# Attention scores as three 32-row products beside the up projection, a turn to the values every two key tiles, and a geglu stage in a written order

## The chip, the cores and the metric

The kernel runs on one core of a Trainium2 chip. The metric is the device time of one execution in microseconds (us). Before the change, three runs took 1081.52, 1082.40 and 1082.88 us; their median is 1082.4.

## The reference

Two branches read the same x (2048 tokens of 448 numbers), and a gate g per token mixes them.

```
q, k, v = split(x @ wqkv)                 # 16 heads of 28
a = softmax(q @ k.T * 28**-0.5) @ v @ wo
b = (gelu(x @ w_gate) * (x @ w_up)) @ w_down      # hidden width 1792
g = sigmoid((x * gate_w).sum(-1, keepdims=True))
out = g * a + (1 - g) * b
```

## The kernel before, in words

All large products but the values' are made in three pieces: each operand is split into a high part (fp32r, TensorE's fast form of fp32) and a low part, and high x high, high x low and low x high are summed. UNITS (line 46) lists the 21 products of 64 rows of which one block of x @ w consists (x has 448 columns: seven pieces of 64 rows, three products each). A block is 128 outputs by 512 tokens.

The program has three stages.

*First* (lines 88 to 265): x, wqkv and the gate vector are loaded and split; q and k are computed and stored to HBM as high and low parts (qkd), v stays in SBUF as V, and per head a shift that keeps exp in range goes to shd. A few warm-up products on zeros (WARM, line 113) run ahead. Then a flag is read and a branch (line 295) is passed that these inputs don't take.

*Attention* (lines 267 to 503): for each head h and each of 16 tiles of 128 keys (kt), two half score tiles of 128 keys by 1024 queries are made. `scores` (line 356) fills a PSUM tile sc (three buffers of two banks) with two 512-column chunks. Q and K of a head lie in SBUF twice, on rows 0 to 63 and on rows 64 to 127: K has high and low part stacked in 28 rows each and a few rows of ones, so one 64-row product makes (K high + K low) x Q high and a second one x Q low. That is four 64-row products per half. ScalarE takes exp of sc into pt (line 378). Four value products per key tile and half pair (`values`, line 381) multiply pt by V, each on its own strip of 32 columns of TensorE, in plain fp32, which the profile shows as two passes each.

Beside the scores the same loop computes x @ w_up, and the first part of x @ w_gate, in blocks of 21 products on one half of the rows (`product`, `unit`, `start`); the result goes from PSUM (psu, one buffer) by a VectorE copy (two buffers u) to HBM (ud). NOUT is the number of blocks made in this stage; a block's half of the rows alternates from block to block. `run` (line 350) writes the order in which the two halves get their products, so that two of them can lie side by side. RATE is the largest number of up products for one half tile. After a block, `hold` keeps the next one back for a few half tiles so that its copy can finish. ENDS and LATE set when the loop turns to the values: a group ends at the key tiles in ENDS, and its values are run when LATE half tiles of the next group are done; then hold is 0 again. Two blocks are made ahead of the loop and two behind it (`two_blocks`), side by side in one score tile. The next head's Q and K are loaded at key tile 2 of each head, all on SP's DMA queue.

*Geglu* (lines 506 to 631): the hidden width is cut in 14 pieces of 128 (ORDER), two to a chunk. `hidden` makes, for each piece and pair of token blocks, the w_gate product if it isn't made yet (pg), then gelu on ScalarE, times u on VectorE, then the split into high and low part hl. `down` multiplies by w_down into pd, and VectorE adds (1 - g) times the result to acc (lines 573 to 578). The projection of the attention output by wo (`project`) is put between. In this stage most instructions of ScalarE, VectorE and SP are placed by the framework's scheduler; only TensorE's products have the order in which they are written (`mm` pins them).

Of the kernel before, what the change touches and what calls it, by code (L numbers as in the profile page):

```python
# [17 lines left out]
P = 128  # L18
# [9 lines left out]
ENDS = (3, 7, 11, 15)  # L28
LATE = 3
RATE = 4  # L30
NOUT = 68
# [4 lines left out]
WARM = 9  # L36
LAG = 6
NR = 2 * DH
# [15 lines left out]
def gated_mix(ctx: ExitStack, tc: tile.TileContext, xT, wqk, wvg, wg, wu, wd, wo, sel, ident, out):  # L54
# [26 lines left out]
    def both(dst, src, mark=lambda ins: ins, eng=None):  # L81

        for g in range(2):
            mark((eng or nc.sync).dma_start(out=dst[side(g), 0:4], in_=src[0:64]))
            mark((eng or nc.sync).dma_start(out=dst[side(g), 4:7], in_=src[64:128, 0:3]))


    with ExitStack() as ph:
# [37 lines left out]
        def load():  # L126
            nonlocal issued
            if issued == len(loads):
                return
            a, r = loads[issued], raws[issued % AHEAD]  # L130
            k = int(a[-1])
            for g in range(2):
                eng = nc.scalar if a in ("x00", "x02") else nc.sync
                if a[0] == "a":
                    src, n = wqk[k, 0:64], TB
                elif a[0] == "b":
                    src, n = wqk[k, 64:128, 0:3 * P], 3 * P
                elif a[0] == "x":
                    src, n = xT[int(a[1]) + 2 * g, side(k // 4), k % 4], TB
                else:  # L140
                    src, n = wvg[side(k // 4), k % 4], VW
                pin(eng.dma_start(out=r[side(g), 0:n], in_=src))
            issued += 1
# [126 lines left out]
    heads = [(kq.tile([P, 2, S], F32R, name=f"Q{i}"), kq.tile([P, S], F32R, name=f"K{i}")) for i in range(2)]  # L270
    for Q, K in heads:
        for g in range(2):
            edge = slice(64 * g + 32, 64 * g + 64)
            pin(nc.gpsimd.memset(K[edge].bitcast(F32), 1.0))
            pin(nc.gpsimd.memset(Q[edge].bitcast(F32), 0.0))

    def load_q(dst, h):
        for a in range(2):
            for g in range(2):
                for j in range(2):  # L280
                    at = 64 * g + j * DH
                    nc.sync.dma_start(out=dst[at:at + DH, a].bitcast(F32), in_=qkd[a, h * DH:(h + 1) * DH])

    def load_k(dst, h):
        for g in range(2):
            for a in range(2):
                at = 64 * g + a * DH
                nc.sync.dma_start(out=dst[at:at + DH].bitcast(F32), in_=qkd[a, D + h * DH:D + (h + 1) * DH])
# [41 lines left out]
    with ExitStack() as ph:  # L330
        pp = ph.enter_context(tc.tile_pool(name="pp", bufs=11))
# [7 lines left out]
        def load_head(h):  # L339
            Q, K = heads[h % 2]  # L340
            if h:
                load_k(K, h)
                load_q(Q, h)
            for g in range(2):
                nc.sync.dma_start(out=Q[64 * g + NR:64 * g + NR + 2, 0].bitcast(F32), in_=shd[h])


        free = [0, 0]

        def run(todo):  # L350
            while todo[0] or todo[1]:
                g = min((g for g in range(2) if todo[g]), key=lambda g: free[g])
                todo[g].pop(0)()
                free[g] = max(free[g], free[1 - g] - 1) + 1

        def scores(h, kt, half, n):
# [3 lines left out]
            todo = [[], []]  # L360
            n = min(n, left())
            if n:

                f = block["g"]
                todo[f] += [unit] * n
                to = (1 - f, 1 - f if n > 1 else f)
            else:
                f = min(range(2), key=lambda g: free[g])
                to = f, 1 - f
            for c in range(2):  # L370
                g = to[c]
                for a in range(2):
# [8 lines left out]
        def values(h, kt):  # L381
            if kt == 0:
                PO[h] = pso.tile([P, 512], F32, name="po")
# [38 lines left out]
        def product(block):  # L422
# [4 lines left out]
            if block["n"] == len(UNITS):  # L427
                u = op.tile([P, TB], F32, name="u")
                nc.vector.tensor_copy(u, block["p"])  # L429
                nc.sync.dma_start(out=block["out"], in_=u)  # L430
# [11 lines left out]
        def unit():  # L442
# [3 lines left out]
            if block["n"] == len(UNITS):  # L446
                hold = 3

        def two_blocks():

            sc = psc.tile([P, 1024], F32, name="sc")
            todo = []
            for g in range(2):
                start(sc[:, g * 512:(g + 1) * 512])
                b = dict(block)
                todo.append([lambda b=b: product(b)] * len(UNITS))
            block["n"] = len(UNITS)
            run(todo)
# [40 lines left out]
        hold = 0  # L499
        while left():  # L500
            unit()
            hold = 0
# [3 lines left out]
    with ExitStack() as ph:  # L506
        ap = ph.enter_context(tc.tile_pool(name="ap", bufs=1, reuse_waits="tile"))
        acc = ap.tile([P, NT, D], F32, name="acc")
        hp = ph.enter_context(tc.tile_pool(name="hp", bufs=8, reuse_waits="tile"))
# [7 lines left out]
        def load_f(f):  # L517
            if any((1, f, tb) not in made for tb in range(NTB)):
                if (1, f) not in halves:
                    load_half(1, f, by_act)  # L520

            hi, lo = 0, TB
            w = gp.tile([P, 2 * TB], F32R, name="w", bufs=3)
            draw = gp.tile([P, TB], F32, name="draw")[:, 0:D]
            nc.sync.dma_start(out=draw, in_=wd[f * P:(f + 1) * P])
            hi, lo = w[:, hi:hi + D], w[:, lo:lo + D]
            nc.scalar.activation(hi, draw, AF.Copy)  # L527
            nc.vector.tensor_tensor(lo, draw, hi.bitcast(F32), OP.subtract)
            WD[f] = hi, lo

        def hidden(f, b):

            us, pgs, hls = [], [], []
            for tb in (b, b + 2):
                s = slice(tb * TB, (tb + 1) * TB)
                u = tp.tile([P, TB], F32, name="u")
                nc.sync.dma_start(out=u, in_=ud[0, f, :, s])
                us.append(u)
                if (1, f, tb) in made:
                    pg = tp.tile([P, TB], F32, name="gs", bufs=2)  # L540
                    nc.sync.dma_start(out=pg, in_=ud[1, f, :, s])
                else:
                    pg = psg.tile([P, TB], F32, name="pg")
                pgs.append(pg)
# [122 lines left out]
```

## Time and profile before

The profiled execution took 1081.29 us; its span, from the first to the last instruction, is 1079.5 us.

| engine | busy us | share of the span |
|---|---|---|
| TensorE products | 1047.9 | 97% |
| TensorE weight loads | 733.0 | 68% |
| ScalarE | 612.3 | 57% |
| VectorE | 332.9 | 31% |
| GpSimd | 69.2 | 6% |

How to read the rows: PE is a TensorE product, PEld a weight load (it overlaps products), DVE is VectorE, ACT ScalarE, POOL GpSimd, SP the engine that issues most DMAs. A group's row gives line, engine, operation, out<-in and count, then the busy time of the group in us and the mean of one in ns, then the idle time of the engine just ahead of them with what ended it. All products have line 60, so the tile's name tells them apart: sc scores, pu up blocks, po values, pg w_gate, pd the second product and the projection. Products are pipelined: one of 512 columns is shown 0.39 us long while the next starts much earlier, so the distance between starts is the price, and "busy" is not work at full rate. A timeline row gives start and length in us.

### The profile page before, as it was taken

What the parts mean: (1) busy time and instruction counts of PE and PEld (TensorE: products, weight loads), DVE (VectorE), ACT (ScalarE), POOL (GpSimd) and SP (SyncE); (2) the same over time, 40 slices, a digit from 0 to 9 for tenths busy, and PEclk for the clock granted to TensorE, in tenths of its full rate; (3) what the DMA queues carried; (4) which work ended last, traced back from release to release, by engine and by line L of the source; (5) the groups of instructions that cost most, each with busy time, mean ns of one, the idle gap of its engine ahead of it and who ended that gap; (6) DMA issues with size and microseconds to landing.
All of it is one profiled execution on the core that took longest, in us unless ns stands there. A gap on an engine that the chain in (4) does not pass through costs nothing.

```text
span 1079.5 us, 20134 instructions
## 1 busy us (share of the span) xinstructions
PE 1047.9 (97%) x8257; PEld 733.0 (68%) x8257; DVE 332.9 (31%) x515; ACT 612.3 (57%) x740; POOL 69.2 (6%) x47
## 2 busy tenths in 40 slices
PE   8999799999999999999999999999888999999997
PEld 6889555655665665565566556556576889888886
DVE  4552112111111111111111111111287656646644
ACT  5332377777777877777787777778344304131320
POOL 3524200000000000000000000000001011100000
PEclk9999899999999999999999999999998999999999
DMA  6795544345345344344354444422476314122313
GB/s 188 250 380 148 133 115 134 106 124 138 103 128 144 89 134 137 102 126 132 101 141 118 111 135 114 123 81 67 152 208 199 103 57 120 49 59 80 105 49 137
DMA packets 68321, 138.19 MB, mean 128 GB/s; under 512 B 15744, under 2 KB 25984, under 8 KB 62784
## 3 DMA queue, kind: packets, MB, share of 16 engines
q1 hardware_dynamic: 67904, 136.33, 42.8%
q8 instruction: 66, 1.08, 0.4%
q10 hardware_dynamic: 320, 0.52, 0.2%
q14 instruction: 31, 0.25, 0.1%
HBM read 96.44 MB, written 40.37 MB: 127 GB/s over the span
## 4 chain that ended last, share of the span: by engine, by line
PE 77%; DMA 4%; ACT 3%; DVE 3%; issue 2%; SPq 0%; DVEq 0%; ACTq 0%
PE po L60 21%; PE sc L60 21%; PE pu L60 16%; PE pd L60 11%; PE pg L60 8%; ACT pt L378 2%; DMA out<-gs 1%; DMA u<-ud 1%; DVE ohl L601 1%; DMA oraw<-in_wo 1%; DVE gs L578 1%; DMA oraw<-od 1%; DMA draw<-in_wd 1%; DVE g L554 0%; DMA gs<-ud 0%
## 5 line engine op out<-in xcount | busy, mean ns | idle before, releaser
L378 ACT ACTIVATE pt<-sc 128x1024 f32<-128x1024 f32 x512 | 477.7, 1041 | 170.6 <-PE sc L60 169.5
L60 PE MATMUL sc<-Q,K 64*128 64x512 f32 x2048 | 413.8, 399 | 0.6 <-ACT pt L378 0.4
L60 PEld LDWEIGHTS sc<-Q,K 64*128 64x128 f32 x2048 | 314.5, 184 | 83.3 <-issue 50.3
L60 PE MATMUL pu<-X,half 64*128 64x512 f32 x1344 | 317.4, 387 | 0.0
L60 PEld LDWEIGHTS pu<-X,half 64*128 64x128 f32 x1344 | 247.1, 184 | 33.9 <-issue 1.7
L60 PE MATMUL po<-pt,V 128*32 128x512 f32 x2048 | 234.4, 598 | 0.0
L60 PE MATMUL pd<-w,hl 128*128 128x448 f32 x672 | 145.5, 373 | 9.8 <-DVE acc L575 5.0
L60 PEld LDWEIGHTS po<-pt,V 128*32 128x32 f32 x2048 | 60.2, 110 | 139.5 <-issue 135.8
L429 DVE COPY u<-pu 128x512 f32<-128x512 f32 x64 | 43.8, 685 | 348.9 <-PE pu L60 289.4
L60 PEld LDWEIGHTS pd<-w,hl 128*128 128x128 f32 x672 | 126.4, 190 | 28.1 <-DVE acc L575 6.2
L60 PE MATMUL pg<-X,half 64*128 64x512 f32 x924 | 106.9, 388 | 0.0
L60 PEld LDWEIGHTS pg<-X,half 64*128 64x128 f32 x924 | 88.1, 184 | 18.5 <-issue 2.7
L60 PE MATMUL pq<-X,WQK 64*128 64x512 f32 x588 | 69.2, 394 | 3.1 <-ACT X L161 2.5
L60 PEld LDWEIGHTS pq<-X,WQK 64*128 64x128 f32 x588 | 56.1, 188 | 16.4 <-ACT X L161 3.3
L527 ACT ACTIVATE w<-draw 128x448 fp32r<-128x448 f32 x14 | 8.1, 578 | 92.8 <-PE pd L60 70.2
L575 DVE SCALAR_TENSOR_TENSOR acc<-pd,gate,acc 128x448 f32<-128x448 f32 x80 | 52.8, 681 | 17.0 <-PE pd L60 16.9
L599 POOL CAST ohl<-oraw 64x512 fp32r<-64x512 f32 x4 | 2.4, 606 | 800.2 <-DMA oraw<-od 698.9
L555 ACT ACTIVATE hl<-g 128x512 fp32r<-128x512 f32 x56 | 33.9, 629 | 24.8 <-DVE g L554 20.6
L554 DVE TENSOR_TENSOR g<-g,u 128x512 f32<-128x512 f32 x56 | 36.7, 687 | 33.3 <-ACT g L553 28.5
L556 DVE TENSOR_TENSOR hl<-g,hl 128x512 fp32r<-128x512 f32 x56 | 36.7, 689 | 9.2 <-ACT hl L555 8.3
L553 ACT ACTIVATE g<-pg 128x512 f32<-128x512 f32 x44 | 24.1, 593 | 26.3 <-PE pg L60 26.3
L60 PE MATMUL pd<-WO,ohl 128*128 128x448 f32 x176 | 36.7, 367 | 0.0
(65 smaller groups left out, 449.2 us busy)
## 6 DMA issues: line engine op xcount, KB each, us to landing
Q<-qkd SPq DMA_DIRECT2D x128, 224.0 KB
ud<-u SPq DMA_DIRECT2D x68, 256.0 KB
qkd<-hl SPq DMA_DIRECT2D x28, 512.0 KB
K<-qkd SPq DMA_DIRECT2D x64, 224.0 KB
u<-ud SPq DMA_DIRECT2D x56, 256.0 KB
rb<-rdend SPq DMA_DIRECT2D x64, 64.0 KB
hraw<-in_wu SPq DMA_DIRECT2D x28, 128.0 KB
od<-o SPq DMA_DIRECT2D x64, 56.0 KB
```

Source lines behind the costliest of these rows:

```text
L60: return pin(nc.tensor.matmul(o, lhsT, rhs, start=start, stop=stop))
L378: nc.scalar.activation(pt, sc, AF.Exp, scale=SCALE)
L429: nc.vector.tensor_copy(u, block["p"])
L527: nc.scalar.activation(hi, draw, AF.Copy)
L553: nc.scalar.activation(g, pg, AF.Gelu_apprx_tanh)
L554: nc.vector.tensor_tensor(g, g, u, OP.mult)
L555: nc.scalar.activation(hl[:, 0], g, AF.Copy)
L556: nc.vector.tensor_tensor(hl[:, 1], g, hl[:, 0].bitcast(F32), OP.subtract)
L575: nc.vector.scalar_tensor_tensor(acc[:, t], p, g1, acc[:, t], OP.mult, OP.add)
L578: nc.vector.scalar_tensor_tensor(y, p, g1, acc[:, t], OP.mult, OP.add)
L599: nc.gpsimd.tensor_copy(O[0:64, 3], o[0:64, 3])
L601: nc.vector.tensor_tensor(O[64:, 3], o[64:, 3], O[64:, 3].bitcast(F32), OP.subtract)
```

## The change

- **Scores.** Q and K are laid out anew: on each quarter of 32 rows K has its high part in one plane and its low part in another (`[P, 2, S]`), and Q holds high and low part for the 512-query chunks of its quarter. A 512-column chunk of scores is three 32-row products (K high x Q high, K low x Q high, K high x Q low) on one quarter; the two chunks take the two quarters of one half of the rows, and the up products the other half. `run` orders three lists by quarters. Six products per half tile take the place of four.
- **Loop.** ENDS is every second key tile, so the values are run for two key tiles at a time, twice as often; LATE is 2 half tiles, RATE 3 up products. The first half tiles of head 0 get one more. `two_blocks` ahead of the loop is gone; behind the loop the unfinished block and one more run side by side, their copies are issued behind both, then come the last values. NOUT is 66 instead of 68. pt has 8 buffers instead of 11.
- **Geglu.** All instructions of the stage are pinned. The parts hl have one place per piece and token block. The gate's tail (gelu, times u, split) is cut into steps; `down` and `project` run one step of waiting side work between the product and the sum of each tile, and the weights, u and gate inputs of the next chunk are prepared in the second half of a chunk. w_down pieces have 4 buffers instead of 3. The split of the attention output moves from GpSimd to ScalarE and VectorE, piece by piece.
- **Elsewhere.** 12 warm-up products instead of 9; loads that went to both halves of the rows as two DMAs are one DMA with a broadcast source; fewer and smaller GpSimd memsets.

The core of the diff (the weights, wo and w_down loads and most of the pins are left out):

```diff
-ENDS = (3, 7, 11, 15)
-LATE = 3
-RATE = 4
-NOUT = 68
+ENDS = tuple(range(1, 16, 2))
+LATE = 2
+RATE = 3
+NOUT = 66
-WARM = 9
+WARM = 12
...
-    heads = [(kq.tile([P, 2, S], F32R, name=f"Q{i}"), kq.tile([P, S], F32R, name=f"K{i}")) for i in range(2)]
+    heads = [(kq.tile([P, 2, 2, TB], F32R, name=f"Q{i}"), kq.tile([P, 2, S], F32R, name=f"K{i}")) for i in range(2)]
...
     def load_q(dst, h):
         for a in range(2):
-            for g in range(2):
-                for j in range(2):
-                    at = 64 * g + j * DH
-                    nc.sync.dma_start(out=dst[at:at + DH, a].bitcast(F32), in_=qkd[a, h * DH:(h + 1) * DH])
+            for g in range(4):
+                nc.sync.dma_start(out=dst[quarter(g, DH), a].bitcast(F32), in_=queries(qkd[a, h * DH:(h + 1) * DH], g))
...
-        free = [0, 0]
+        free = [0] * 4
 
         def run(todo):
-            while todo[0] or todo[1]:
-                g = min((g for g in range(2) if todo[g]), key=lambda g: free[g])
-                todo[g].pop(0)()
-                free[g] = max(free[g], free[1 - g] - 1) + 1
+            todo = [(q, list(p)) for q, p in todo if p]
+            now = 0
+            while todo:
+                q, p = min(todo, key=lambda a: max(free[i] for i in a[0]))
+                now = max(now, *(free[i] for i in q))
+                p.pop(0)()
+                for i in q:
+                    free[i] = now + 1
+                todo = [a for a in todo if a[1]]
...
-                f = block["g"]
-                todo[f] += [unit] * n
-                to = (1 - f, 1 - f if n > 1 else f)
+                g = block["g"]
+                todo.append(((2 * g, 2 * g + 1), [unit] * n))
+                to = 2 - 2 * g
             else:
-                f = min(range(2), key=lambda g: free[g])
-                to = f, 1 - f
+                to = min((0, 2), key=lambda g: max(free[g:g + 2]))
             for c in range(2):
-                g = to[c]
-                for a in range(2):
-                    todo[g].append(lambda g=g, a=a, c=c: mm(
-                        sc[:, c * 512:(c + 1) * 512], K[side(g), kt * P:(kt + 1) * P],
-                        Q[side(g), a, half * 1024 + c * 512:half * 1024 + (c + 1) * 512], a == 0, a == 1))
+                r = quarter(to + c, 32)
+                todo.append(((to + c,), [lambda a=a, b=b, r=r, c=c: mm(
+                    sc[:, c * 512:(c + 1) * 512], K[r, a, kt * P:(kt + 1) * P], Q[r, b, half],
+                    a + b == 0, b == 1) for a, b in ((0, 0), (1, 0), (0, 1))]))
             run(todo)
...
         def values(h, kt):
+            free[:] = [max(free)] * 4
...
         load_head(0)
-        two_blocks()
...
-                    spaced(h, kt, half, 0 if due and count == LATE or count == LATE + 1 and h + kt > 3 else RATE)
+                    spaced(h, kt, half, RATE + (h == 0 and kt <= ENDS[0] + 1))
...
-        hold = 0
-        run([[], [unit] * left()] if block.get("g") else [[unit] * left(), []])
-        while NOUT - 1 - block["at"] >= 2:
-            two_blocks()
+        rest = [dict(block)]
+        if block["at"] + 1 < NOUT:
+            start(psc.tile([P, 1024], F32, name="sc")[:, 0:512])
+            rest.append(dict(block))
+        run([((2 * b["g"], 2 * b["g"] + 1), [lambda b=b: product(b)] * (len(UNITS) - b["n"])) for b in rest])
+        for b in rest:
+            put(b)
         for a in due:
             values(*a)
...
+        def tails(f, i, tbs, pgs):
+            a, b = (tail(f, i, tb, pg) for tb, pg in zip(tbs, pgs))
+            return [a[0], b[0], a[1], b[1]]
...
+        def step():
+            if side_work:
+                side_work.pop(0)()
...
+                step()
                 g1 = gate[:, 2, t:t + 1]
...
+        for n, chunk in enumerate(chunks):
+            nxt = chunks[n + 1] if n + 1 < len(chunks) else ()
+            for b in range(2):
+                for i, f in enumerate(chunk):
+                    if not here(f, b):
+                        if (n, b) not in early:
+                            for a in tails(f, i, (b, b + 2), (None, None)):
+                                a()
+                    else:
+                        side_work += gate_blocks(f, i, b)
+                        if (b, i) != (1, FC - 1):
+                            while side_work:
+                                step()
...
+            for k, tb in enumerate((0, 2, 1, 3)):
+                if (n, k) == (1, 1):
+                    side_work += load_o(0)
+                down(n, tb, chunk)
...
+                if nxt and k == 1:
+                    side_work += [lambda f=f: prepare(f) for f in nxt]
+                    for i, f in enumerate(nxt):
+                        if not here(f, 0):
+                            side_work += tails(f, i, (0, 2), (None, None))
+                            early[n + 1, 0] = 1
```

More of the change, by code (lines that the diff above doesn't have):

```diff
@@ L426, in product, with put @@
             mm(block["p"], block["w"][r, w], X[r, x, block["s"]], block["n"] == 1, block["n"] == len(UNITS))
[L427 to L430, printed above, removed]
+        def put(block):
+            u = op.tile([P, TB], F32, name="u")
+            nc.vector.tensor_copy(u, block["p"])
+            nc.sync.dma_start(out=block["out"], in_=u)
         def left():
@@ L446, in unit @@
             if block["n"] == len(UNITS):
+                put(block)
                 hold = 3
[L449 to L458, printed above, removed]
         hold = 0
```

228 lines of the change are left out of this document (109 added, 119 removed).

## The prediction

> **What bounds the kernel now.** I read the page's head first, then the busy time by stretches, then the groups of instructions and the chain of waits, and last the timeline of a few microseconds of attention.
>
> ```profile
> span 1079.5 us, 20134 instructions
> ```
>
> ```profile
> 119.20:126.40 7.20, 6.39 (x41) 5.25 (x41) 0.69 (x1) 0.00 (x0) 0.00 (x0) 0.80 0.00 1
> 130.00:760.00 630.00, 629.38 (x5364) 377.73 (x5362) 92.97 (x142) 473.41 (x510) 0.00 (x0) 1.00 0.42 117
> 776.20:850.00 73.80, 64.73 (x380) 54.20 (x378) 53.75 (x79) 28.01 (x45) 4.07 (x2) 0.95 0.55 168
> 850.00:1079.00 229.00, 222.02 (x1400) 193.27 (x1396) 132.81 (x190) 59.88 (x97) 12.32 (x6) 1.00 0.28 86
> ```
>
> The columns of the stretches are TensorE products, weight loads, VectorE, ScalarE, GpSimd, then granted clock, DMA share and GB/s. In attention (130 to 760) TensorE is busy 629.4 of 630 us at full clock, with ScalarE at 473 and DMA at 0.42. There only fewer, or better packed, TensorE slots can help. From 776 to 850 TensorE is idle 9 us and its clock drops to 0.95; that stage has waits to win. After 850 it has few.
>
> The groups, and the chain's two neighbouring turns to the values:
>
> ```profile
> L378 ACT ACTIVATE pt<-sc 128x1024 f32<-128x1024 f32 x512 | 477.7, 1041 | 170.6 <-PE sc L60 169.5 <-ACT pt L378 1.1
> L60 PE MATMUL sc<-Q,K 64*128 64x512 f32 x2048 | 413.8, 399 | 0.6 <-ACT pt L378 0.4
> L60 PE MATMUL pu<-X,half 64*128 64x512 f32 x1344 | 317.4, 387 | 0.0
> L60 PEld LDWEIGHTS sc<-Q,K 64*128 64x128 f32 x2048 | 314.5, 184 | 83.3 <-issue 50.3 <-ACT pt L378 6.8
> L60 PE MATMUL po<-pt,V 128*32 128x512 f32 x2048 | 234.4, 598 | 0.0
> L60 PE MATMUL pd<-w,hl 128*128 128x448 f32 x672 | 145.5, 373 | 9.8 <-DVE acc L575 5.0 <-DVE acc L573 3.6 <-DVE hl L556 0.7
> L60 PE MATMUL pg<-X,half 64*128 64x512 f32 x924 | 106.9, 388 | 0.0
> L429 DVE COPY u<-pu 128x512 f32<-128x512 f32 x64 | 43.8, 685 | 348.9 <-PE pu L60 289.4 <-DMA K<-qkd 55.4 <-PE sc L60 4.0
> L60 PEld LDWEIGHTS pr<-selt,sq 128*1 128x1 f32 x14 | 0.4, 81 | 0.0
> ```
>
> ```profile
> 405.75 3.57 PE po L60 x32
> ...
> 415.68 3.57 PE po L60 x32
> ```
>
> A group of four key tiles (eight half score tiles, one turn to the values) takes 415.68 - 405.75 = 9.93 us. Inside it the timeline of products shows the slot:
>
> ```profile
> 410.96 0.39 PE L60 MATMUL sc<-Q,K 64*128 64x512 f32 x1
> 410.97 0.39 PE L60 MATMUL pu<-X,half 64*128 64x512 f32 x1
> ...
> 414.36 0.39 PE L60 MATMUL sc<-Q,K 64*128 64x512 f32 x1
> 414.37 0.39 PE L60 MATMUL pu<-X,half 64*128 64x512 f32 x1
> 414.59 1.10 PE L60 MATMUL sc<-Q,K 64*128 64x512 f32 x7
> 415.61 3.64 PE L60 MATMUL po<-pt,V 128*32 128x512 f32 x32
> 419.18 0.50 PE L60 MATMUL sc<-Q,K 64*128 64x512 f32 x2
> ```
>
> and that of weight loads shows what lies side by side:
>
> ```profile
> 411.19 0.18 PEld L60 LDWEIGHTS sc<-Q,K 64*128 64x128 f32 x1
> 411.20 0.18 PEld L60 LDWEIGHTS pu<-X,half 64*128 64x128 f32 x1
> ...
> 416.07 0.13 PEld L60 LDWEIGHTS po<-pt,V 128*32 128x32 f32 x4 [0.30 <-issue]
> ...
> 418.21 0.13 PEld L60 LDWEIGHTS po<-pt,V 128*32 128x32 f32 x4 [0.30 <-issue]
> ```
>
> A score product and an up product start 0.01 us apart on the two halves of the rows, and the next pair comes (414.36 - 410.96) / 15 = 0.2267 us later: this is my **slot**. Four value products lie side by side on four column strips, and the next four come (418.21 - 416.07) / 5 = 0.428 us later. The group adds up: 32 score and 21 up products are 26.5 slots, 6.01; eight fours of values are 3.42; 0.50 is left for the two switches of shape and for slots with one side empty.
>
> **The loop, after.** A half score tile is now six products, three in a row on each of two quarters, and at most three up products on the other half of the rows: three slots. I followed the loop's own rules for hold. From the second group on they repeat every eight halves: seven with three up products (one block of 21), one with none, which still takes three slots, and the turn after it sets hold to 0. So there are 512 x 3 = 1536 slots, and 5 more because the first five halves get a fourth up product. Those products that are no longer in the two blocks ahead of the loop ride in it for nothing: the score chain sets the slot.
>
> The slot's price is the unknown, as no row shows 32-row products, or two sizes at once. Nearest is the 64-row pair, same data, same 128-column load: 0.2267, which I take. Its low end is 0.214, half of the value fours' 0.428 (two passes of 512 columns at half rate); its high end I put at 0.25, a tenth over the pair, since three loads, each 0.18 long, must start in one slot rather than two. 1541 x 0.2267 = 349.3 (ends 330 and 385).
>
> Values: 127 turns in the loop of four fours each, 127 x 4 x 0.428 = 217.4; the same work as before. But there are twice as many turns. Leaving values costs 419.18 - 415.61 - 3.42 = 0.15; entering them, one pair and seven single products (4.5 slots, 1.02) take 415.61 - 414.36 = 1.25, so 0.23. I take 0.38 per turn, 48.3 in all; ends 0.15 (19) and the whole remainder 0.50 (64).
>
> Every second half without up products puts its scores on rows where up products just ran (the choice falls on the lower pair when both are equally free): 32 changes of size on the same rows, 0 to 0.23 each, I take 3. Loop: 349.3 + 217.4 + 48.3 + 3 = 618.0. Before, it ran from 126.43 to 762.04, 635.6 (rows below). **-17.6.**
>
> Cover for what I cost at nothing: ScalarE needs 477.7 / 512 = 0.933 per half, 3.73 of a group's 4.81 (12 slots, four fours, 0.38). A turn needs the exp of the half scored 1.36 us before it: it starts about 0.2 after that score's last 0.39, waits for one exp in front, and lies some 0.9 us ahead of the fours that read it; rival A is that this is wrong. SP's loads per head go from 14 to 20 issues of the same size in all (4 + 8 loads of 224 KB become 8 of 224 and 8 of 112), with some 38 us to land. Behind them on SP queues the store of the up block, whose buffer (two) the VectorE copy needs, and the next block needs the copy. From a block's last product to the next one's first there are a slot, a half and a turn, 3.0 us; the copy takes 0.39 and 0.69, which leaves 1.9. GpSimd's smaller memsets free nobody in attention.
>
> **Around the loop.**
>
> ```profile
> 119.18 6.41 PE L60 MATMUL sc<-X,half 64*128 64x512 f32 x41 [6.11 <-DVEq L295]
> 126.43 0.49 PE L60 MATMUL sc<-X,half 64*128 64x512 f32 x1 [0.84 <-DVE u L429]
> ...
> 762.04 0.49 PE L60 MATMUL sc<-X,half 64*128 64x512 f32 x1
> ...
> 770.29 0.94 PE L60 MATMUL sc<-X,half 64*128 64x512 f32 x2 [2.89 <-DVE u L429]
> 771.16 5.06 PE L60 MATMUL po<-pt,V 128*32 128x512 f32 x32
> 776.15 9.83 PE L60 MATMUL pg<-X,half 64*128 64x512 f32 x84
> ```
>
> Ahead: the two blocks from 119.18 to 126.43, 7.25, go. The branch that ends at 119.18 stays, and so does the low clock after it (0.80 over 7.2 us, 1.4 lost), which now falls on scores. **-5.8.**
>
> Behind: 762.04 to 776.15, 14.1, with a wait of 2.9 on a copy out of the same score tile and values at a low clock (5.06 for what takes 3.57). After: 21 slots for the last two blocks together, a switch, four fours: 4.76 + 0.38 + 1.71 = 6.85, and the copies stand behind the products. **-7.3**; 0 if the values wait for those copies.
>
> The rest (geglu): 66 blocks made ahead instead of 68, so 42 products more on w_gate, 21 slots, +4.8. Of the waits of the second product (9.8 idle in its row, nearly all in 776 to 850) the longest came so:
>
> ```profile
> 827.18 0.69 DVE L554 TENSOR_TENSOR g<-g,u 128x512 f32<-128x512 f32 x1 [3.70 <-DMA u<-ud]
> ```
>
> VectorE stood at a product whose u had not landed, with the sums of the second product behind it, and TensorE behind those. In the written order u is asked for two tiles of work ahead and one small step goes between two sums. The memory for the first w_down pieces now comes free with the last score, not with the last value, and 16 us (6.85 and the first 9.5 of w_gate) hide the two loads. I let 2 of the 9.8 stay, and half of the 3.7 that the clock of 0.95 costs over 73.8. -7.8 - 1.8 + 4.8: **-4.8**, ends -9 and +5. What is late next is the sum's own pace, then the stores at the very end, as before.
>
> The kernel's start (three more warm-up products, half as many load issues): 0 to -3, I take **-1**.
>
> Sum: -17.6 - 5.8 - 7.3 - 4.8 - 1 = -36.5 on the span of 1079.5, 1043.0. The profiled run took 1081.29, 1.8 more than its span, and the median of the runs is 1.1 above that: **1046** us.
>
> **Rivals.** *A, the turn waits for ScalarE.* With LATE 2 the values follow their last exp by two halves, 1.36 us and one key tile's values. For it: TensorE makes a half in 0.68, ScalarE takes 0.93. Against it: ScalarE idled 169.5 us waiting for scores, and its share becomes 3.73 of 4.81. Each 0.1 per turn is 12.7 us; at 0.2 the time is 1071, from 0.29 on nothing is won. Slots of 0.24 give about the same (+20). Chance 0.19: 0.15 faster, 0.02 same, 0.02 slower.
>
> *B, products of 32 and 64 rows don't run side by side.* Then the change doesn't do what it says. Every change of shape in this trace (0.15 and 0.23 above) stops the flow, though there the new shape needs rows or columns of the old one, and here it doesn't; all that lies side by side in the trace is of one shape. Each of some 1350 slots with an up product would be two, with two switches: 0.2267 + 0.38 more, +820, some 1866 us. It decides as soon as a slot costs 0.024 more. Chance 0.09.
>
> The Trainium skill, "TensorEngine Tiling (Array Packing)", section Key Properties, states this rule: changing the tiling mode, and not just the tile, drains TensorE. By it the sum would be rival B's; the trace agrees for shapes that share rows, and has no row for shapes that don't.
>
> *C, the third weight load makes the slot.* A load of one column takes 81 ns and one of 128 takes 184, so 103 is the columns; three, one after another, are 0.309 per slot: +0.082 x 1541 = 127, about 1173. It decides from 0.25. Against it: two loads start 0.01 apart and each takes 0.18, and four small ones end within 0.13. Chance 0.06.
>
> **How the numbers follow.** Forecast 0.66, A 0.19, B 0.09, C 0.06. The low end takes the slot at 0.214 (-19) and keeps the rest: 1027, say 1028. The high end, 1080, takes in A up to 0.27 per turn, and leaves out B, C and what is left of A. A measurement of this kernel tells 0.2%, 2 us. Faster 0.81, same 0.02, slower 0.17.
>
> **What would show it.** Right: three starts (one up product, two scores) every 0.227 us; 4.8 us from turn to turn; 3072 score products, 966 on w_gate; values about 7 us behind the last score; no wait over 1 us between 740 and 810. Wrong: up and score starts alternating with 0.2 and more between (B); an even slot of 0.3 (C); value products that wait for exp at each turn (A); a wait on VectorE in the second product as large as before.

## The result: 2922.2 us, 2.70 times the time before

Four runs of the changed kernel took 2920.99 to 2923.40 us, median 2922.16. Four runs of the kernel before had a median of 1082.64, so the ratio is 2.698 (95% interval 2.693 to 2.703). The forecast was 1046 us with a range of 1028 to 1080, and no case named in it reached this time. The profiled execution took 2920.99 us.

The page of the changed kernel, its head and the rows of TensorE's busy share and granted clock (40 slices, tenths):

```profile
span 2919.2 us, 22114 instructions
...
PE   3567999999999999999999999999999999658887
...
PEclk6786555555555555555555555555555555778999
```

TensorE is still always busy in the middle, but at little over half the clock, and at both ends it now waits. By stretches (products, weight loads, VectorE, ScalarE, GpSimd, granted clock, DMA share, GB/s):

```profile
0.00:100.00 100.00, 41.60 (x186) 27.40 (x188) 13.85 (x22) 15.51 (x26) 12.07 (x14) 0.65 0.13 49
...
1000.00:1500.00 500.00, 500.00 (x1449) 181.72 (x1449) 19.19 (x29) 115.89 (x114) 0.00 (x0) 0.58 0.10 31
...
2521.30:2919.00 397.70, 305.46 (x1814) 262.80 (x1814) 186.56 (x287) 93.96 (x157) 0.00 (x0) 0.87 0.28 88
```

Where the 1839.7 us between the two spans went, from the starts of the first score, the last score and the first w_gate product of geglu:

| stretch | before | after | difference |
|---|---|---|---|
| start, to the first score | 126.8 | 261.0 | +134.3 |
| attention, to the last score | 634.8 | 2235.8 | +1600.9 |
| to the first product on w_gate | 14.6 | 24.5 | +9.9 |
| geglu, to the end | 303.4 | 397.9 | +94.6 |

The groups that answer to those of before:

```profile
L59 PE MATMUL sc<-Q,K 32*128 32x512 f32 x3072 | 1035.6, 707 | 14.4 <-DMA Q<-shd 14.4
L59 PE MATMUL pu<-X,half 64*128 64x512 f32 x1365 | 959.7, 706 | 0.0
L384 ACT ACTIVATE pt<-sc 128x1024 f32<-128x1024 f32 x512 | 520.5, 1023 | 1730.6 <-PE sc L59 1712.7
...
L59 PE MATMUL po<-pt,V 128*32 128x512 f32 x2048 | 446.3, 1021 | 0.0
...
L59 PE MATMUL pd<-w,hl 128*128 128x448 f32 x672 | 154.3, 391 | 56.0 <-DVE acc L601 48.6
...
L59 PE MATMUL pg<-X,half 64*128 64x512 f32 x966 | 116.3, 399 | 44.2 <-ACT half L328 38.3
```

A score product is shown 707 ns long, where it was 399, and an up product 706 instead of 387. ScalarE waits 1713 us for scores, so it is not what sets the turn (rival A). The timeline of products says what the slot has become; the first rows are at half clock, the last at full:

```profile
1500.15 0.80 PE L59 MATMUL sc<-Q,K 32*128 32x512 f32 x2
1500.88 0.79 PE L59 MATMUL pu<-X,half 64*128 64x512 f32 x1
1501.60 0.79 PE L59 MATMUL sc<-Q,K 32*128 32x512 f32 x2
...
1512.23 0.49 PE L59 MATMUL sc<-Q,K 32*128 32x512 f32 x2
1512.65 0.49 PE L59 MATMUL pu<-X,half 64*128 64x512 f32 x1
1513.07 0.50 PE L59 MATMUL sc<-Q,K 32*128 32x512 f32 x2
```

This is the picture that the prediction named for rival B. The two quarter products of scores start together ("x2"), but at full clock an up product starts only 0.42 us after them and they 0.42 us after it. A slot, from one pair of scores to the next, is 0.84 us at full clock in these rows (0.86 in the median over attention, so 0.43 from start to start) and 1.45 at half, where the sum had 0.2267.

The start: the queue of SP as it issues the loads of x and w (start, length), and what the first products wait for:

```profile
1.51 10.28 SPq L138 DMA_DIRECT2D raw<-in_xT  x2
11.84 8.71 SPq L138 DMA_DIRECT2D raw<-in_wqk  x1
20.59 14.15 SPq L138 DMA_DIRECT2D raw<-in_xT  x3
```

```profile
16.39 1.65 PE L59 MATMUL pq<-X,WQK 64*128 64x512 f32 x6 [9.45 <-ACT X L157]
24.66 2.93 PE L59 MATMUL pq<-X,WQK 64*128 64x512 f32 x12 [6.62 <-ACT X L157]
```

Issues of these loads hold SP 4 to 5 us each (median of raw<-in_xT 5.03 and of raw<-in_wqk 4.43, before 0.594 for both), and the DMA share of the first 100 us is 0.13. There are half as many, but they carry the same bytes and follow one another slowly. Not all of them are broadcasts, as the list of the change has it: one DMA of raw<-in_wqk reads the same 64 rows twice, while one of raw<-in_xT reads two different blocks of 64 rows for the two halves. What they share is an outer dimension of two, and both are slow.

### The profile page after: what moved, and what is told of

Same layout as the page of the kernel before. It is cut to its first block, busy times and chain, and to the rows that moved or that the text cites. A ratio compares the mean times of both kernels' runs of the same rounds, so it can differ in the third digit from the quotient of the medians.

```text
span 2919.2 us, 22114 instructions
## 1 busy us (share of the span) xinstructions
PE 2696.2 (92%) x9284; PEld 1200.1 (41%) x9284; DVE 329.8 (11%) x529; ACT 660.0 (23%) x752; POOL 42.3 (1%) x37
## 4 chain that ended last, share of the span: by engine, by line
PE 84%; DMA 5%; DVE 2%; SPq 1%; issue 1%; ACT 0%; DVEq 0%; ACTq 0%
PE sc L59 32%; PE pu L59 30%; PE po L59 15%; PE pd L59 3%; PE pg L59 3%; DMA hraw<-in_wg 3%; DMA out<-gs 1%; DMA r<-dend 0%; DVE acc L601 0%; DMA K<-qkd 0%; DMA gs<-ud 0%; ACT half L328 0%; DVE gs L604 0%; DVE w L520 0%; DVE half L224 0%
## 5 line engine op out<-in xcount | busy, mean ns | idle before, releaser
L59 PE MATMUL sc<-Q,K 32*128 32x512 f32 x3072 | 1035.6, 707 | 14.4 <-DMA Q<-shd 14.4
L59 PE MATMUL pu<-X,half 64*128 64x512 f32 x1365 | 959.7, 706 | 0.0
L384 ACT ACTIVATE pt<-sc 128x1024 f32<-128x1024 f32 x512 | 520.5, 1023 | 1730.6 <-PE sc L59 1712.7
L59 PEld LDWEIGHTS pu<-X,half 64*128 64x128 f32 x1365 | 349.8, 257 | 661.9 <-issue 660.3
L59 PEld LDWEIGHTS sc<-Q,K 32*128 32x128 f32 x3072 | 396.0, 264 | 537.7 <-issue 523.8
L59 PE MATMUL po<-pt,V 128*32 128x512 f32 x2048 | 446.3, 1021 | 0.0
L59 PE MATMUL pq<-X,WQK 64*128 64x512 f32 x588 | 98.7, 496 | 91.5 <-ACT X L157 34.9
L59 PE MATMUL pq<-WV,X 64*128 64x450 f32 x336 | 40.5, 398 | 8.4 <-DVE gate L196 8.4
L59 PEld LDWEIGHTS pq<-WV,X 64*128 64x128 f32 x336 | 37.0, 210 | 11.4 <-DVE gate L196 9.4
L224 DVE TENSOR_TENSOR half<-hraw,half 128x896 fp32r<-128x896 f32 x29 | 31.6, 1091 | 79.7 <-ACT half L328 79.1
```

What stands on the lines that cost most here:

```text
L59: return pin(nc.tensor.matmul(o, lhsT, rhs, start=start, stop=stop))
L224: mark(nc.vector.tensor_tensor(w[:, NS:], raw, w[:, 0:NS].bitcast(F32), OP.subtract))
L384: nc.scalar.activation(pt, sc, AF.Exp, scale=SCALE)
```

## The experiments

Two theories stood at the start. *Drain*: two products of different row counts don't run side by side even on rows that they don't share; TensorE empties at each change. *Third load*: weight loads, or the third product in a slot, are the limit, whatever the size. Beside them stood the question of the clock, and the two ends of the kernel, which the prediction had priced as small gains. Where no ratio is given a kernel ran once; the kernel before took 1081 to 1087 us beside these runs, so differences of tens of us can be read.

**a_two_loads.** The changed kernel with the loads to both halves of the rows as two DMAs again, in the start, for the pieces of w_up and w_gate and in geglu (the helper `both` and the load of the attention output are left out here):

```diff
-                src = src.unsqueeze(0).to_broadcast([2, 64, n])
-            pin(eng.dma_start(out=r[:, 0:n], in_=src))
+            for g in range(2):
...
+                pin(eng.dma_start(out=r[side(g), 0:n], in_=src))
```

> The changed kernel with each load to both halves of the rows issued as two DMAs again, as before. Theory: the one-DMA form with an outer dimension of two is what slows the start (first score at 261 us in place of 127), the wait ahead of w_gate and the geglu stage (398 us in place of 303); the attention loop is untouched. Expected: loop still some 2236 us, start back to about 125, geglu to about 300, in all about 2685 us. Rival: the written order, not the loads, slows the geglu stage; then it stays near 398 and the time is about 2780.

It took 2718.1 us. Stretches of its start and attention:

```profile
0.00:100.00 100.00, 96.29 (x838) 79.25 (x840) 46.22 (x88) 38.63 (x72) 36.49 (x34) 1.00 0.77 248
120.50:2354.60 2234.10, 2234.10 (x6451) 814.98 (x6451) 92.40 (x142) 520.10 (x512) 0.00 (x0) 0.57 0.12 33
```

The first score starts at 120.5 instead of 261.0, the attention keeps its length (2234.1 us), and geglu falls from 397.9 to 344.3, not to the 300 expected: it lies between the two cases, and the written order has a part of its own (c_new_geglu). So the loads cost some 200 of the 1840 us and have nothing to do with the slot.

**b_broadcast.** The other way round: the kernel before with only its loads changed to one DMA with an outer dimension of two (a broadcast for the weights, two blocks of rows for x; the helper `both` and the other sources are left out here).

```diff
-            for g in range(2):
...
-                pin(eng.dma_start(out=r[side(g), 0:n], in_=src))
...
+                src = src.unsqueeze(0).to_broadcast([2, 64, n])
+            pin(eng.dma_start(out=r[:, 0:n], in_=src))
```

> The kernel before with nothing but its loads changed to the one-DMA form. Theory: the start grows by some 115 us and w_gate waits for its weights, up to 95 us more: 1195 to 1290 us, with the DMA share near two engines of sixteen (0.13) while they run. Rival: the form of the load costs nothing by itself and only the order around it did: 1082 us.

It took 1261.57 us, with runs of the kernel before at 1081 to 1086 beside it. Stretches of its start, attention and geglu:

```profile
0.00:100.00 100.00, 38.63 (x181) 25.11 (x183) 13.85 (x22) 15.51 (x26) 12.08 (x14) 0.65 0.13 49
261.90:898.70 636.80, 635.20 (x5402) 381.70 (x5404) 92.99 (x143) 476.98 (x513) 0.00 (x0) 1.00 0.42 117
914.90:1259.00 344.10, 299.50 (x1776) 257.78 (x1772) 185.69 (x269) 87.68 (x142) 16.39 (x8) 0.93 0.31 94
```

The start is as slow as in the changed kernel (DMA share 0.13, 49 GB/s; with two loads, in a_two_loads, 0.77 and 248), attention is untouched, and geglu is 41 us longer. This edit alone, a tidy-up in appearance, costs some 177 us.

**c_new_geglu.** The kernel before up to the end of attention, then the changed kernel's written geglu, with two loads.

```diff
+                step()
...
-                    nc.vector.scalar_tensor_tensor(acc[:, t], p, g1, acc[:, t], OP.mult, OP.add)
+                    pin(nc.vector.scalar_tensor_tensor(acc[:, t], p, g1, acc[:, t], OP.mult, OP.add))
...
+        def prepare(f):
+            if here(f, 1):
+                load_half(1, f, by_act, pin)
+            load_w(f)
...
+                    side_work += [lambda f=f: prepare(f) for f in nxt]
```

> Start and attention of the kernel before, the geglu stage of the changed kernel, with loads to both halves as two DMAs. The prediction's term for this stage, without its two blocks more: 303 us become about 294, so 1073 us. Rival: the written order blocks VectorE as long as the scheduler's order did: 1082; or longer: above 1090.

It took 1112.81 us, the median of five runs, ratio 1.0271 (1.0248 to 1.0293). From the first w_gate product to the end geglu takes 327.4 us, not 303.4, with the same 924 products on w_gate. One of its five waits on these sums (17.5 us in all), in order of time, ScalarE, VectorE and then TensorE:

```profile
892.94 0.95 ACT L327 ACTIVATE half<-hraw 128x896 fp32r<-128x896 f32 x1 [7.86 <-DMA hraw<-in_wg]
893.92 1.09 DVE L228 TENSOR_TENSOR half<-hraw,half 128x896 fp32r<-128x896 f32 x1 [4.44 <-ACT half L327]
```

```profile
896.20 5.49 PE L60 MATMUL pd<-w,hl 128*128 128x448 f32 x18 [3.71 <-DVE acc L604]
```

A step of side work (`prepare`) issues the load of a w_gate piece and its split together. The split's second half is on VectorE, so VectorE stands until the load has landed, with the sums of the second product behind it in the written order, and TensorE runs out of places for results.

**d_up32.** a_two_loads with the up products on 32 rows (half of their contraction is left out), so that all three products of a slot have one size:

```diff
-            r = side(block["g"])
+            r = quarter(2 * block["g"], 32)
```

> The changed kernel with two-DMA loads, whose up products use only 32 of their 64 rows, so half of that contraction is left out; every product in the loop but the values then has 32 rows. Theory (products of different row counts do not overlap, and the clock falls because TensorE then looks half idle): one size side by side, a slot of 0.227, clock 1.0, loop about 618 us, total about 1050. Rival C (three loads in a slot): slot 0.3 or more, loop above 730, total above 1160. Rival (any change of place in the array drains): as slow as with 64 rows, about 2685.

It took 1122.23 us. Timeline of products and stretch of attention:

```profile
403.35 0.39 PE L59 MATMUL pu<-X,half 32*128 32x512 f32 x1
403.35 0.40 PE L59 MATMUL sc<-Q,K 32*128 32x512 f32 x2
403.58 0.39 PE L59 MATMUL pu<-X,half 32*128 32x512 f32 x1
403.58 0.39 PE L59 MATMUL sc<-Q,K 32*128 32x512 f32 x2
```

```profile
120.70:763.60 642.90, 634.42 (x6450) 345.84 (x6453) 93.00 (x142) 481.90 (x512) 0.00 (x0) 0.99 0.41 115
```

Three products with three loads start within 0.01 us, and the next three 0.23 us later. That is the forecast's slot, so *third load* (rival C too) falls and *drain* stands: the only difference to a_two_loads is the row count of one of three products. What is shown is that products of two sizes wait for each other; that the array runs empty in between can't be seen in a profile that models the ends of products. The time missed the 1050 expected, as the loop took 643 us instead of 618 and geglu 341, where the forecast's term (303.4 less 4.8) leaves 299.

**e_three_then_three.** a_two_loads with the three up products of a half tile ahead of its six score products, so that the size changes twice per half tile and not six times:

```diff
-                q, p = min(todo, key=lambda a: max(free[i] for i in a[0]))
+                q, p = todo[0] if len(todo[0][0]) == 2 else min(todo, key=lambda a: max(free[i] for i in a[0]))
```

> The changed kernel with two-DMA loads, whose half tiles run their three up products first and their six score products after them, not in turn: two changes of row count per half in place of six. Theory (a change of row count lets TensorE run empty, some 0.2 us each): 1.76 us per half in place of 2.58 at full clock, loop about 1090 and total about 1575 if the clock stays at 1.0, since TensorE then streams 1.36 of 1.76; if the clock stays at 0.57 all the same, about 2200. Rival (32-row products are slow beside or after 64-row ones whatever the order): 2700 as now.

It took 1990.25 us; the median turn is 10.86 us (17.87 in the changed kernel), the clock in attention 0.65. At full clock:

```profile
407.88 0.97 PE L59 MATMUL sc<-Q,K 32*128 32x512 f32 x6
408.78 0.96 PE L59 MATMUL pu<-X,half 64*128 64x512 f32 x3
409.67 0.96 PE L59 MATMUL sc<-Q,K 32*128 32x512 f32 x6
```

Three slots of one size and one change take 0.89 us; three slots are 0.68, so a change costs 0.21 us here. In the changed kernel it is 0.43 - 0.23 = 0.20. The price goes with the number of changes. A half tile thus takes 1.79 us at full clock, where 1.76 was expected; the time lies between the two cases named, as the clock did.

**g_up32_three.** e_three_then_three with up products of 32 rows as in d_up32 (half of the contraction left out). It was to tell whether the low clock comes from the drains or from rows that do nothing.

> As e_three_then_three (two loads, each half tile three up products and then six score products), but the up products have 32 rows as the scores have; half of the up products' contraction is left out. One size everywhere, so nothing drains, yet only some of the rows are busy at a time. If the clock of e (0.65 in the loop) falls because TensorE runs empty at each change of size, it stays near 1.0 here: three up products in a row (0.2267 apart or less, on one quarter) and then six scores on two quarters give some 5 to 6.5 us from turn to turn, a loop of 650 to 850 and about 1130 to 1330 us. If it falls because few rows are busy, it is about 0.65 again, with turns near 10 us and about 1900 us.

It took 1125.97 us at a clock of 0.99, but it did not tell what it was made for. The program has three up products and then six scores; the trace has them side by side all the same:

```profile
403.31 0.38 PE L59 MATMUL pu<-X,half 32*128 32x512 f32 x1
403.32 0.39 PE L59 MATMUL sc<-Q,K 32*128 32x512 f32 x2
403.53 0.38 PE L59 MATMUL pu<-X,half 32*128 32x512 f32 x1
403.55 0.39 PE L59 MATMUL sc<-Q,K 32*128 32x512 f32 x2
```

Products of one size on different rows don't wait for each other here, so as much of the array was at work as in d_up32. It confirms d_up32: with one size the order hardly matters, with two sizes it decides.

**j_scores_alone** and **k_one_quarter** asked for the clock again, without any change of size. The first is d_up32 with 20 of each 21 up products left out; the second also puts both chunks of scores on one quarter.

```diff
-            mm(block["p"], block["w"][r, w], X[r, x, block["s"]], block["n"] == 1, block["n"] == len(UNITS))
+            if block["n"] == 1:
+                mm(block["p"], block["w"][r, w], X[r, x, block["s"]], True, True)
```

and in k_one_quarter also

```diff
-                r = quarter(to + c, 32)
-                todo.append(((to + c,), [lambda a=a, b=b, r=r, c=c: mm(
+                r = quarter(to, 32)
+                todo.append(((to,), [lambda a=a, b=b, r=r, c=c: mm(
```

> d_up32 with 20 of the 21 products of each up block left out: in the loop the scores run alone on two quarters, one half of TensorE's rows, and nearly no two sizes meet. It asks what halves the clock when two sizes alternate. If it is that half of the rows or more do nothing, the clock falls here too, towards 0.57 to 0.65, the slot becomes up to 0.45 and the turn 7 to 9 us: 1400 to 1700 us in all. If it is that TensorE drains at each change of size, there is no drain here and the clock stays at 0.98 to 1.0, with the turn at 4.9 us and 1115 to 1135 us in all.

> j_scores_alone with both chunks of scores on one quarter, so that three quarters of the rows do nothing (the second chunk takes the same queries as the first). The products follow each other without a change of size: six slots to a half tile, 24 to a turn. If a drain is what lowers the clock, it stays at 0.98 to 1.0 even so: turns of 24 x 0.2267 + 1.7 + 0.46 = 7.6 us, a loop of some 975 and about 1460 us in all. If the share of busy rows is what lowers it, the clock is at 0.5 to 0.6 and the turn at 11 to 14 us, 1900 to 2300 us in all.

They took 1213.1 and 1968.72 us. The attention of each:

```profile
136.00:854.00 718.00, 687.40 (x5164) 353.34 (x5166) 92.58 (x142) 485.89 (x511) 0.00 (x0) 0.91 0.35 102
```

```profile
136.40:1612.00 1475.60, 1475.60 (x5167) 843.18 (x5168) 92.47 (x142) 522.66 (x512) 0.00 (x0) 0.59 0.17 50
```

In k_one_quarter TensorE is busy all of 1475.6 us, no size changes but at the turns to the values, and still the clock is 0.59, so changes of size are not needed for a low clock. For each kernel I worked out what share of the array its attention uses per granted cycle: scores and up products at 0.2267 us times their share of the rows, the values at 0.428 us for four (the whole array), over the loop's time times its clock. For the changed kernel: (3072 x 0.25 + 1365 x 0.5) x 0.2267 + 512 x 0.428 = 548 us, over 2235.8 x 0.573.

| kernel | share of the array used | granted clock |
|---|---|---|
| changed kernel | 0.43 | 0.57 |
| k_one_quarter | 0.45 | 0.59 |
| e_three_then_three | 0.56 | 0.65 |
| j_scores_alone | 0.60 (0.63 between its waits) | 0.91 (1.00) |
| d_up32, g_up32_three | 0.74 | 0.99 |
| before | 0.95 | 1.00 |

k_one_quarter came out as the theory of busy rows had it (0.59, a turn of 11.2 us). j_scores_alone did not, though its mean of 0.91 and its 1213 us lie between the two cases. In attention TensorE waits there once in each of 14 heads:

```profile
PE pu L59 <- DVE u L438: 30.6, 14, 3.1
```

These waits are 1.5 to 3.1 us long. After its first 12 us, every stretch of half clock in this attention (14 of them, 3.4 to 17 us) begins within 3 us of the end of one of them. The 95 turns of 127 that lie wholly at full clock take 4.90 us each, as in d_up32, with 24 score products and four fours of values: (24 x 0.25 x 0.2267 + 4 x 0.428) / 4.90 = 0.63 of the array. So the tenth lost belongs to these waits, and half of the rows left idle did not lower the clock by itself. In d_up32, with 0.74, waits of up to 1.5 us were not followed by half clock; one of 2.0 was, for 3.4 us.

Of the kernels in which TensorE waits less than 1 us inside the loop, those with 0.43 to 0.56 of the array in use fell to 0.57 to 0.65 of the clock, and the kernel before with 0.95 did not; j_scores_alone puts the border, if it is this share that counts, above 0.56 and not above 0.63. That a change of size lowers the clock by leaving the array empty fits the table, but was not tried by itself. What exactly is counted (rows, or products per time) these runs don't tell.

**f_fetch_ahead** and **h2_entry** went after geglu. The first is c_new_geglu with the w_gate and w_down pieces fetched one block of tokens ahead of their split, into buffers of their own, and the first w_gate piece asked before attention ends. The second also moves the last head's multiply by its reciprocal row to GpSimd, and asks for the attention output behind the next chunk's preparation (first lines f_fetch_ahead, last two h2_entry; the buffers and the move of the load are left out):

```diff
+                if nxt and k == 0:
+                    for f in nxt:
+                        fetch(f)
...
-            nc.vector.tensor_tensor(o, o, rb, OP.mult)
+            (nc.vector if h < H - 1 else nc.gpsimd).tensor_tensor(o, o, rb, OP.mult)
```

> As c_new_geglu (start and attention of before, the written geglu order), but the w_gate and w_down pieces of the next chunk are asked for one tile block earlier, in two buffers each, and the first w_gate piece before the attention ends. Theory: the 30 us by which the written order lost come from a step that holds a load, its split on ScalarE and on VectorE in one, with the sums behind it: the waits of 17.5 (second product) and 13.2 (w_gate) us go, about 1083 us, and with the old waits of the stage gone too perhaps 1075. Rival: the steps between the sums cost by themselves; then it stays above 1100.

> The kernel before with the written order of geglu and its pieces fetched one tile block earlier (f_fetch_ahead), and two more moves: the multiply of the last head's attention output by its reciprocal row goes from VectorE to GpSimd, so that the split of the first w_gate piece no longer stands behind a DMA on VectorE, and the first load of the attention output is asked after the next chunk's preparation and not ahead of it. If the waits of f (8.4 at its entry, 4.6 at 846) are the causes read from its trace, both go or halve, the clock behind them stays full, and the time falls from 1086.7 to 1072 to 1080, below both kernels. If these waits only covered the next one (the u or w loads), another wait of the same size appears in the same place and the time stays at 1084 to 1087.

f_fetch_ahead took 1086.72 us, ratio 1.0019 (1.0006 to 1.0032): the loss of c_new_geglu is nearly gone, and two waits of TensorE are left that matter. Before the first of them VectorE stood at the last head's multiply:

```profile
787.55 0.69 DVE L404 TENSOR_TENSOR o<-o,rb 128x512 f32<-128x512 f32 x1 [6.68 <-DMA rb<-rdend]
```

```profile
790.69 1.84 PE L60 MATMUL pd<-w,hl 128*128 128x448 f32 x3 [7.65 <-ACT hl L553]
...
846.41 6.69 PE L60 MATMUL pd<-w,hl 128*128 128x448 f32 x24 [4.56 <-DVE acc L615]
```

h2_entry took 1076.03 us, ratio 0.9936 (0.9918 to 0.9953), below both kernels and inside what was expected. Its two longest waits of TensorE in geglu:

```profile
786.38 0.47 PE L60 MATMUL pd<-w,hl 128*128 128x448 f32 x1 [2.32 <-ACT hl L553]
...
799.28 15.07 PE L60 MATMUL pd<-w,hl 128*128 128x448 f32 x72 [2.71 <-DVE acc L613]
```

7.65 became 2.32 and the wait of 4.56 is gone, while one of 0.81 ahead of the same 72 products became 2.71. Geglu takes 298.2 us where it took 303.4 before, and starts 10.8 us behind the last score where it was 14.6. A written order of this stage can win, here once these instructions that waited for a DMA no longer stood ahead of the sums.

## Why the prediction was wrong, point by point

**The slot is the step that failed.** "Nearest is the 64-row pair, same data, same 128-column load: 0.2267, which I take", with ends of 0.214 and 0.25. The price holds for three products of 32 rows (d_up32), not for two sizes. The low and high ends came from rows of one size, so the range held only the doubt about three loads, which was none. The chain's account by line in the changed kernel, shares of 2919.2 us:

```profile
PE sc L59 32%; PE pu L59 30%; PE po L59 15%; PE pd L59 3%; PE pg L59 3%; DMA hraw<-in_wg 3%; DMA out<-gs 1%; DMA r<-dend 0%; DVE acc L601 0%; DMA K<-qkd 0%; DMA gs<-ud 0%; ACT half L328 0%; DVE gs L604 0%; DVE w L520 0%; DVE half L224 0%
```

Scores and up products hold 62%, 1810 us, where the sum had 349.3 + 3; the values 15%, 438, where it had 217.4 + 48.3.

**Rival B was the mechanism, and its price was short.** It had the loop at 618 + 820 = 1438 us. At full clock that was nearly right: 1365 slots of 0.86 are 1174, and with 176 free slots (40), values (217) and turns (48) the loop would be 1479. It took 2236, 1.51 times that, as the clock was 0.57. Of the 1056 us by which 1866 missed, 757 are thus the clock, 41 the slot, and the rest the start, the tail and geglu. Its chance of 0.09 was set by the argument that shapes which share no rows need not wait for each other; no row of the trace bore that out, while both changes of shape that it showed (0.15 and 0.23) stopped the flow. The Trainium skill, "TensorEngine Tiling (Array Packing)", section Key Properties, says that a change of tiling mode, not just of tile, drains TensorE. a_two_loads against d_up32 agrees, for tiles that share no rows: 0.86 against 0.23 us a slot.

**The clock had no term.** The prediction read 1.00 in attention and carried it over. By the Trainium skill, "TensorE: Matmul & The Clock Gate", Part 1, the clock is full or half, chosen by how busy TensorE was in windows of 3.41 us. The trace agrees: in the attention of the changed kernel the stretches of one clock are whole multiples of 3.41 us, 3.4 at full and nearly all 10.2 to 34.1 at half. But idle gaps, which the same part gives as what brings the half clock, are not needed: the stretch from 1000 to 1500 shows none. The runs point to the small share of the array in use instead: k_one_quarter has nearly the same share and clock without the changes of size.

**The start, -1.** "Half as many load issues" counted issues, not what one issue takes: +134 us to the first score, of which a_two_loads takes back all (140, as the first score then comes ahead of that of the kernel before). The Trainium skill, "DMA: Bandwidth & Descriptors", section Rules for kernel authors, says that an outermost dimension of size c under 16, a leading broadcast of c copies for one, keeps a DMA on at most c engines. The share of 0.13 over the first 100 us, in which loads of both kinds run (x, and the broadcast ones), agrees with two of sixteen (0.125).

**Ahead of the loop, -5.8**, was about right: with two loads the first score starts 6.3 us earlier than before (120.5 against 126.8), where this term and the start's -1 had 6.8.

**The rest of the loop** can be judged in d_up32. The turn is 4.90 us; less 12 slots (2.72) and four fours (1.71) that leaves 0.47 for the two switches, not 0.38: +11 us. The cover named for the store of the up block ("leaves 1.9") was too thin. Once in most heads VectorE's copy waits for the store of an earlier block, and weight loads of the up products wait for the copy (total, times, longest):

```profile
DVE u L437 <- DMA ud<-u: 148.9, 13, 12.9
...
PEld pu L59 <- DVE u L437: 21.0, 14, 2.9
```

The loop is 643.0 us, 16 more than 128 turns of 4.90. It does not beat the 634.8 of before even with a slot of 0.2267, so the -17.6 would have failed without any drain. ScalarE as the limit (rival A) did not appear.

**Behind the loop, -7.3.** The products came as forecast: in d_up32 the last four values start 6.4 us behind the last score, for an end of the values at 6.85. But the first product on w_gate starts 9.0 us after that, as its weights are not there (14.76 us of waiting in the changed kernel). The prediction did not ask what would be late next; f_fetch_ahead asks for that piece earlier, and the wait is gone.

**Geglu, -4.8.** "One small step goes between two sums" took the step for small. A step that holds a load and its split holds VectorE as long as the load takes. The written order alone cost 24 us (c_new_geglu). The changed kernel's geglu with two loads takes 17 more (344.3): 4.8 of these are the two blocks, 6.7 a wait for the w_gate pieces of the third chunk, and the rest was not taken apart. The slow loads added 54, and with them the same pieces came 23.5 us late:

```profile
2628.02 0.80 PE L59 MATMUL pg<-X,half 64*128 64x512 f32 x2 [23.49 <-ACT half L328]
```

So four terms of the sum besides the slot (the turns, behind the loop, geglu and the start) had the wrong size or sign, and d_up32, with the slot right, is at 1122 us still slower than before.

## What to carry to other kernels

Pack small products side by side only in one size, and test a mix of two sizes in a few microseconds of timeline before building on it; where the size must change, let it change seldom. A price taken from one clock is worth nothing if the change leaves part of the array idle: ask what share of it is at work. In an order written by hand, keep an instruction that waits for a DMA out of the queue that frees the bottleneck's results, and fetch one step earlier. Time a tidy-up of loads by itself: one DMA with an outer dimension of two in place of two DMAs cost 177 us here (b_broadcast).

## What the runs showed of the hardware that was not expected

- A change between products of 64 and of 32 rows costs 0.20 to 0.21 us at full clock, though the two share no rows; without one, three products of 32 rows start within 0.01 us.
- TensorE that is shown busy without a gap can run at 0.57 to 0.65 of its clock: 0.43 to 0.56 of the array in use per granted cycle was not enough, while 0.63 (j_scores_alone between its waits) and 0.74 (d_up32) kept the full clock.
- With 0.63 in use, waits of 1.5 to 3.1 us were each followed by half clock, mostly for 6.8 us (j_scores_alone).
- With one size, products written three up, then six scores, ran as if they had been written in turns (g_up32_three).
- One DMA with an outer dimension of two (a broadcast of 64 rows to both halves, or two blocks of rows) took SP 4.4 to 5.0 us to issue instead of 0.594, and the start moved 49 GB/s, against 248 with two DMAs.
